# Moving the scan of later batches, its decay matmul, pair 2's loads and four half tiles in a fused state-space and feed-forward kernel

One core of a Trainium2 chip. The metric is the device time of one execution in microseconds (us); the profiled span is about 1.7 us shorter than it. In the views PE is TensorE (PEld its weight loads), DVE is VectorE, ACT is ScalarE, POOL is GpSimd and SP the queue that issues most loads; to turn means to transpose, to evict means to copy a result out of PSUM, and a load lands when its last byte is there.

## The reference

Two stages. The first is a chunked state-space scan over `x, a, B, C` (4 batches, 8 heads, 768 steps, head width 32, state width 16); the second is a gated feed-forward layer over its output, turned to 3072 tokens by 256.

```python
cum = np.cumsum(la, axis=-1)                       # la = log of the decay a, per chunk
M = np.einsum('bhin,bhjn->bhij', Cc, Bc) * np.exp(cum_i - cum_j) * causal
y = einsum(M, xc) + einsum(Cc, state) * np.exp(cum)
state = exp(sum(la)) * state + sum_j(Bc * xc * exp(cum_last - cum))
...
gate = np.maximum(x @ w_gate, 0.0)                 # 256 -> 1536
return (gate * (x @ w_val)) @ w_out                # 1536 -> 256
```

## The kernel before

Tokens go in pairs of 128-token chunks (`p` = 0 to 11). Pairs 0 and 1 belong to batch 0 and must be through before the feed-forward layer has anything to do; pairs 2 and 3 are done between its tiles. For each pair: scale B and C by decay factors, turn them on PE, G = C·B on PE, mask G on DVE, then D = masked G times x on PE, then evict y into `yT`. The decay factors of batch 0 come from a short scan (`cp0`, `fac`), those of the later batches from a 384-long scan of `a_sb` and fp32 matmuls (`decay`). `gvh` is one half tile of gate and value (256 tokens), `gv` a full one; f0 to f5 are the half tiles of tiles 0 to 5. `keep_warm` puts matmuls on zeros into PE's queue, to keep it busy.

```python
    def load_bc(p, j, *qs):
        ...
            if p == 2:
                nc.vector.memset(s["bcr"][0:1, 0, 1, 0, 0:1], 0.0)   # holds the load back
        ...                                                          # till VectorE is here
    def gmask(p, q, eng, psum=False):
        eng.tensor_tensor(out=d, in0=s["gp"][q] if psum else d, in1=m, op=ALU.mult)
    ...
    # front (cut)
    d = factors();  decays(0);  keep_warm(8)
    nc.vector.tensor_copy(wfac[:, 1], d)
    nc.vector.memset(wg[0:1, 0, 0:1], 0.0)        # holds the weight loads back
    weights(0, 2);  weights(2, 4);  weights(4, 6, (0,))
    scale_wide(0, 1, V)
    ...
    scan(0, H)                                     # ahead of pair 0's masks
    scale_wide(1, 1, P_);  scale_wide(1, 0, P_)
    weights(4, 6, (1,))
    ...
    D_wide(0, (2, 3, 0));  D_wide(0, (1,))
    turn(1, True);  keep_warm(2)
    yevac_wide(0, A_, V)
    load_bc(2, 1, nc.sync);  load_bc(2, 0, nc.sync)     # <- pair 2's C and B, here
    carry(0, 1)
    weights(6, 8);  weights(8, NF)
    weights_out(0, NF // 2);  weights_out(NF // 2, NF)
    tevac(1, V, A_);  cast_x(1, V);  pass_on(0, 1)
    f0 = gvh(0, 0, 0, True)
    G_wide(1)
    decay()
    adds(1)
    ...                                            # masks, carry, f0()
    late = [gvh(0, f, 0, True) for f in (1, 2, 3)]
    inter_wide(1);  D_wide(1)
    late[0]();  late[1]()
    yevac_wide(1, A_, V)
    late += [gvh(0, f, 0, True) for f in (4, 5)]
    ...
    scale_wide(2, 1, P_);  scale_wide(2, 0, P_)    # GpSimd, then its masks and memsets
    ...
    halves(0, 1, 0, 1, 2, 3, 4, 5)
    gv(0, 6);  carry(1, 1);  gv(0, 7);  load_x(2, nc.sync);  load(3)
    ...
    gv(0, 8);  turn(2)
```

## Time and profile before

| | before |
|---|---|
| time, median of the first 3 runs | 124.58 us (124.43 to 124.73) |
| profiled span | 122.7 us |
| PE's share of the chain that ended last | 92% |
| PE without a hole from | 14.87 us |
| second halves of the first tiles start | 15.75 us |

The prediction shows the lines that carry this. Two further views matter later. The first is the instructions on pair 2's `bcr` (its B and C) in the stretch where they are asked for: duration (min/median/max ns), first and last start, and the us from issue to landing.

```profile
L89 SPq DMA_DIRECT2D bcr<-in_C_dram x1: 368/368/368, 10.4 to 10.4; - x1
L89 SPq DMA_DIRECT2D bcr<-in_B_dram x1: 995/995/995, 10.8 to 10.8; - x1
DMA to landing us min/median/max: 3.5/4.3/5.2
```

They are issued at 10.4 and 10.8 and are there by 16. The second is busy time by stretch (stretch, length, then busy us and count of PE, weight loads, DVE, ACT and POOL, then granted clock, DMA share, GB/s):

```profile
22.00:24.00 2.00, 2.00 (x12) 0.97 (x11) 1.43 (x4) 1.73 (x4) 0.65 (x2) 1.00 1.14 210
32.00:34.00 2.00, 2.00 (x50) 1.73 (x48) 2.00 (x6) 1.83 (x6) 1.75 (x3) 1.00 0.96 120
```

PE is full in both.

### The profile page before, as it was taken

Reading aid. Unit: us, or ns where it says so; the run is one execution under the profiler, and the core shown is the slowest. Engines: PE = TensorE matmul, PEld = TensorE weight load, DVE = VectorE, ACT = ScalarE, POOL = GpSimd, SP = SyncE. Lnnn points to the kernel's source line nnn. Section 1 sums busy time; section 2 is a strip of 40 time slices with the busy share of each in tenths; the row PEclk is TensorE's granted clock in tenths of the full one; section 3 lists DMA queues with packets and bytes.
Section 4 is the critical chain, followed back from the end, with each engine's and each line's share of the span. In section 5 each row is a group of like instructions: output and inputs, shape, how many; then the busy total and the mean of one; then the engine's idle time right before and its main releaser. Section 6 shows DMA issues by size and latency. Waiting matters only on the chain.

```text
span 122.7 us, 3665 instructions
## 1 busy us (share of the span) xinstructions
PE 118.1 (96%) x1404; PEld 82.4 (67%) x1404; DVE 88.0 (72%) x200; ACT 76.3 (62%) x169; POOL 48.2 (39%) x108
## 2 busy tenths in 40 slices
PE   6989999999999999999999999999999999999990
PEld 6856784577875478874577864677854678844790
DVE  4798988872799864988763897855987656788410
ACT  0467688835987725786635886545877447876420
POOL 6499989361455127360351806033600033000000
DMA  3999999996979995999999498960580002200022
GB/s 63 220 208 146 171 192 194 189 172 103 115 89 139 143 142 143 103 150 205 150 114 140 154 136 138 110 117 0 189 52 0 0 0 91 85 0 0 0 91 86
DMA packets 77489, 13.93 MB, mean 113 GB/s; under 512 B 70064, under 2 KB 77472, under 8 KB 77472
## 3 DMA queue, kind: packets, MB, share of 16 engines
q1 hardware_dynamic: 70128, 10.61, 54.2%
q0 software_dynamic: 4288, 2.36, 14.1%
q10 hardware_dynamic: 3056, 0.72, 2.7%
q8 instruction: 11, 0.18, 0.6%
q14 instruction: 6, 0.05, 0.1%
HBM read 11.13 MB, written 3.15 MB: 116 GB/s over the span
## 4 chain that ended last, share of the span: by engine, by line
PE 92%; POOL 4%; DVE 1%; issue 1%; DVEq 0%
PE o L713 26%; PE gv L686 21%; PE gate L668 15%; PE val L671 15%; PE y L643 2%; PE g L548 2%; PE w L189 2%; POOL wg L199 2%; POOL bs L322 1%; PE y L632 1%; PE o L707 1%; PE A_ps L601 1%; PE g L418 1%; POOL wv L199 1%; PE y L523 1%; PE dec L262 1%
## 5 line engine op out<-in xcount | busy, mean ns | idle before, releaser
L675 DVE TENSOR_TENSOR h<-r,val 128x512 bf16<-128x512 bf16 x44 | 30.0, 685 | 7.3 <-ACT r L674 7.2
L713 PE MATMUL o<-wo,h 128*128 128x256 bf16 x276 | 33.1, 273 | 0.0
L674 ACT ACTIVATE r<-gate 128x512 bf16<-128x512 f32 x44 | 26.3, 597 | 9.7 <-PE gate L668 9.3
L713 PEld LDWEIGHTS <-h 128*128 128x128 bf16 x276 | 25.9, 98 | 5.3 <-issue 1.7
L668 PE MATMUL gate<-yT,wg 128*128 128x512 bf16 x88 | 26.2, 379 | 0.0
L671 PE MATMUL val<-yT,wv 128*128 128x512 bf16 x88 | 26.2, 379 | 0.0
L692 DVE TENSOR_TENSOR h<-r,gv 128x256 bf16<-128x256 bf16 x56 | 22.5, 419 | 2.6 <-ACT r L689 1.8
L689 ACT ACTIVATE r<-gv 128x256 bf16<-128x256 f32 x56 | 21.2, 386 | 2.3 <-PE gv L686 0.2
L686 PE MATMUL gv<-yT,wg 128*128 128x256 bf16 x112 | 21.5, 273 | 0.0
L686 PE MATMUL gv<-yT,wv 128*128 128x256 bf16 x112 | 21.4, 273 | 0.0
L556 POOL TENSOR_SCALAR_AFFINE_SELECT gs<-gs 128x512 bf16<-128x512 bf16 (+1 forms) x16 | 8.0, 523 | 30.0 <-ACT gs L567 30.0
L573 DVE TENSOR_TENSOR gs<-g,maskUT 128x512 bf16<-128x512 f32 x16 | 10.3, 685 | 11.4 <-issue 5.6
L338 POOL TENSOR_TENSOR tok<-bcr,scaleBC 128x128 bf16<-128x128 f32 x32 | 12.2, 409 | 14.1 <-DMA bcr<-in_B_dram 13.0
L671 PEld LDWEIGHTS <-wv 128*128 128x128 bf16 x88 | 8.6, 98 | 10.4
L668 PEld LDWEIGHTS <-wg 128*128 128x128 bf16 x88 | 8.6, 98 | 8.9
L686 PEld LDWEIGHTS <-wv 128*128 128x128 bf16 x112 | 11.0, 98 | 1.3
L686 PEld LDWEIGHTS <-wg 128*128 128x128 bf16 x112 | 10.2, 98 | 1.9 <-DVE yT L536 0.2
L567 ACT CAST gs<-g 128x512 bf16<-128x512 f32 x8 | 4.7, 589 | 6.7 <-PE g L548 6.7
L656 ACT CAST yT<-y 128x512 bf16<-128x512 f32 x8 | 4.7, 586 | 5.1 <-PE y L643 2.5
L433 DVE TENSOR_TENSOR gs<-g,wmask 128x512 bf16<-128x512 f32 x9 | 5.9, 680 | 2.6 <-PE g L418 2.6
L189 PE MATMUL w<-warm 128*128 128x128 bf16 x49 | 5.5, 284 | 1.1 <-DVE tmask L163 1.1
L189 PEld LDWEIGHTS <-warm 128*128 128x128 bf16 x58 | 5.0, 126 | 1.7 <-DVE tmask L163 1.1
(122 smaller groups left out, 115.8 us busy)
## 6 DMA issues: line engine op xcount, KB each, us to landing
xr<-in_x_dram SPq DMA_DIRECT2D x17, 128.0 KB, 3.2
out_dram<-ob SPq DMA_DIRECT2D x3, 512.0 KB, 3.2
bcr<-in_C_dram SPq DMA_DIRECT2D x17, 64.0 KB, 2.9
bcr<-in_B_dram SPq DMA_DIRECT2D x17, 64.0 KB, 2.9
out_dram<-ob SPq DMA_DIRECT2D x4, 256.0 KB, 3.5
xr<-in_x_dram SPq DMA_DIRECT2D x3, 256.0 KB, 4.1
wo<-in_moe_w_out_dram POOLq DMA_DIRECT2D x2, 384.0 KB, 8.5
wg<-in_moe_w_gate_dram POOLq DMA_DIRECT2D x4, 128.0 KB, 4.0
```

Source lines behind the costliest of these rows:

```text
L189: nc.tensor.matmul(out=w, lhsT=warm, rhs=rhs, start=True, stop=True)
L338: eng.tensor_tensor(out=dst[:, t, j * (1 + t)], in0=src[:, j, :, t], in1=f[:, j, :, 4 * t:4 * t + 4].to_broadcast([128, 2, 4, N]), op=ALU. ...
L556: nc.gpsimd.affine_select(out=dst, in_=dst, pattern=[[0, n], [1, 128]], compare_op=ALU.is_ge, fill=0.0, base=0, channel_multiplier=-1)
L573: nc.vector.tensor_tensor(out=d[:, q], in0=g[q], in1=m, op=ALU.mult)
L668: nc.tensor.matmul(out=g, lhsT=wg[:, k, fs], rhs=yT[:, k, tk], start=(k == 0), stop=(k == 1))
L671: nc.tensor.matmul(out=v, lhsT=wv[:, k, fs], rhs=yT[:, k, tk], start=(k == 0), stop=(k == 1))
L674: nc.scalar.activation(r, g, AF.Relu)
L675: nc.vector.tensor_tensor(out=fst[b][:, f], in0=r, in1=v, op=ALU.mult)
L686: nc.tensor.matmul(out=gv_[:, j], lhsT=w[:, k, fs], rhs=yT[:, k, tk], start=(k == 0), stop=(k == 1), skip_group_check=True)
L689: nc.scalar.activation(r, gv_[:, 0], AF.Relu)
L692: nc.vector.tensor_tensor(out=fst[b][:, f, u * 256:(u + 1) * 256], in0=r, in1=gv_[:, 1], op=ALU.mult)
L713: nc.tensor.matmul(out=o[:, ts % 2], lhsT=fst[b][:, f, ts * 128:(ts + 1) * 128], rhs=wo[:, f], start=(f == 0), stop=(f == NF - 1), skip_gr ...
```

## The change

As the diff reads, it means to take the long scan off DVE ahead of pair 0's masks and put it into DVE's waits; to take the fp32 decay matmuls out of the stretch before pair 1's D; to fill that stretch with half tiles f1 to f4 instead, f1 in the PSUM bank that the turns use; and to do tile 5 as a full tile. The diff, cut to its core:

```diff
-    a_sb = glob.tile([2 * BH, H], FP32)                 # before x(0) on the queue
-    nc.sync.dma_start(out=a_sb, in_=a.rearrange(...))
+    a_sb = glob.tile([RL, H], FP32)                     # 48 rows, batches 1 to 3
     load_x(0, nc.sync, nc.scalar)
     load_bc(1, 1, nc.sync)
     load_bc(1, 0, nc.scalar)
+    nc.sync.dma_start(out=a_sb, in_=a[1:].rearrange(...))
@@ decay: d3 in two matmuls of 128 columns instead of four of 64; 48 columns for 64
@@ middle
-        nc.vector.tensor_scalar_mul(pick[:, 0], pairs[:, 0], rmid)
+        nc.scalar.mul(pick[:, 0], pairs[:, 0], rmid)
@@ front
-    keep_warm(8)
-    nc.vector.tensor_copy(wfac[:, 1], d)
+    keep_warm(6)                                        # weight loads asked for before this
     scale_wide(0, 1, V)                                 # now reads fac in PSUM
-    nc.vector.reciprocal(wfac[:, 0, :, :, 0], wfac[:, 1, :, :, 0])
+    nc.vector.reciprocal(wfac[:, 0, :, :, 0:2], fac[:, :, :, 0:2])
+    nc.scalar.copy(out=wfac[:, 1], in_=fac)
...
-    scan(0, H)
+    cast_x(0, A_)
     scale_wide(1, 1, P_)
     scale_wide(1, 0, P_)
-    weights(4, 6, (1,))                                 # all six now ahead of scale_wide(1)
+    cast_x(1, P_)
@@ pair 0's masks: two from ScalarE copies (bf16) instead of one
-    middle()
+    scan(0, H // 2)
...
     yevac_wide(0, A_, V)
-    load_bc(2, 1, nc.sync)
-    load_bc(2, 0, nc.sync)
+    tevac(1, None, A_)
     carry(0, 1)
+    copy_B(1, V)
+    scan(H // 2, H)
     weights(6, 8)
     ...
     G_wide(1)
-    decay()
     adds(1)
     gcopy(1, 0)
-    gmask(1, 2, V, True)
-    f0()
+    gmask(1, 3, V, True)
     gcopy(1, 1)
-    gmask(1, 3, V, True)
+    gmask(1, 0, V)
+    gcopy(1, 2)
+    load_bc(2, 1, nc.sync)
+    load_bc(2, 0, nc.sync)
     carry(1, 0)
-    ...
-    late = [gvh(0, f, 0, True) for f in (1, 2, 3)]
+    gmask(1, 1, V);  pass_on(0, 1);  f0();  pass_on(1, 0);  gmask(1, 2, V);  middle()
+    late = [gvh(0, 1, 0, True, mm.tile(..., tag="tp", name="gv1"))]
+    late += [gvh(0, f, 0, True) for f in (2, 3, 4)]
+    late[0]()
     inter_wide(1)
     D_wide(1)
-    late[0]()
     late[1]()
     yevac_wide(1, A_, V)
-    late += [gvh(0, f, 0, True) for f in (4, 5)]
+    decay()
...
-    halves(0, 1, 0, 1, 2, 3, 4, 5)
-    gv(0, 6)
+    halves(0, 1, 0, 1);  decay_factors();  halves(0, 1, 2, 3, 4)
+    carry(1, 1);  gv(0, 5);  gv(0, 6)
```

More of the change, by code (lines that the diff above doesn't have):

```diff
@@ L138 @@
     load_bc(0, 0, nc.sync, nc.scalar)
-    a_sb = glob.tile([2 * BH, H], FP32)
-    nc.sync.dma_start(out=a_sb, in_=a.rearrange("b h (w s) -> (b h w) s", w=2))
+    RL = 2 * (NB - 1) * NH
+    a_sb = glob.tile([RL, H], FP32)
     load_x(0, nc.sync, nc.scalar)
@@ L143 @@
     load_bc(1, 0, nc.scalar)
+    nc.sync.dma_start(out=a_sb, in_=a[1:].rearrange("b h (w s) -> (b h w) s", w=2))
     load_x(1, nc.sync)
@@ L176 @@
     cp0 = glob.tile([R, 128], FP32)
-    pick = const.tile([2 * BH, 2, BH], FP32)
-    pairs = identf.rearrange("p (h w) -> p w h", w=2)
+    pick = const.tile([RL, 2, RL // 2], FP32)
+    pairs = identf[0:RL, 0:RL].rearrange("p (h w) -> p w h", w=2)
     nc.vector.tensor_copy(pick[:, 1], pairs[:, 1])
@@ L232, in decays @@
         nc.scalar.copy(out=dec, in_=d)
-    cp = glob.tile([2 * BH, H], FP32)
-    rmid = const.tile([2 * BH, 1], FP32)
+    cp = glob.tile([RL, H], FP32)
+    rmid = const.tile([RL, 1], FP32)
     def scan(s0, s1):
@@ L238, in scan @@
             out=cp[:, s0:s1], data0=a_sb[:, s0:s1],
-            data1=zero1.to_broadcast([2 * BH, s1 - s0]),
+            data1=zero1[0:RL].to_broadcast([RL, s1 - s0]),
             initial=cp[:, s0 - 1:s0] if s0 else 1.0, op0=ALU.mult, op1=ALU.add)
@@ L249, in decay @@
     def decay():
-        bank_ = mm.tile([128, HC * 2 * NB * 8 + 16], FP32, tag="tp", name="dec")
-        n = HC * 2 * NB * 8
-        d = bank_[:, 0:n].rearrange("p (k w b h) -> p k w b h", k=HC, w=2, b=NB)
-        st["dec3"] = d3 = bank_[:, n:n + 16].rearrange("p (r h) -> p r h", r=2)
-        for r in range(2):
-            for i in range(2):
-                nc.tensor.matmul(
-                    out=d3[64 * i:64 * i + 64, r], lhsT=cp[:, i * 128 + r:i * 128 + 128:2],
-                    rhs=pick[:, 0, NH:2 * NH], start=(r == 0), stop=True,
-                    tile_position=(0, 64 * i), skip_group_check=True)
+        n = HC * 2 * (NB - 1) * NH
+        bank_ = mm.tile([128, n + 2 * NH], FP32, tag="tp", name="dec")
+        d = bank_[:, 0:n].rearrange("p (k w b h) -> p k w b h", k=HC, w=2, b=NB - 1)
+        st["dec3"] = d3 = bank_[:, n:].rearrange("p (r h) -> p r h", r=2)
+        turned = cp[:, 0:256].rearrange("p (i m r) -> p r i m", i=2, r=2)
+        for r in range(2):
+            nc.tensor.matmul(
+                out=d3[:, r], lhsT=turned[:, r], rhs=pick[:, 0, 0:NH], start=(r == 0),
+                stop=True, skip_group_check=True)
         for k in range(HC):
@@ L274, in decay_factors @@
             nc.scalar.copy(
-                out=scaleBC[:, :, cs, 1, :].rearrange("p b k h -> p k b h"), in_=d[:, :, w])
+                out=scaleBC[:, 1:, cs, 1, :].rearrange("p b k h -> p k b h"), in_=d[:, :, w])
     def inverse(b0, b1):
@@ L319, in scale_wide @@
         src = s["bcr"].rearrange("s (t q) j r n -> s j r t q n", t=2)[:, j]
-        f = wfac[:, j, :, :, p]
+        f = fac[:, :, :, 0] if p == 0 and j else wfac[:, j, :, :, p]
         for t in range(2):
@@ L371, in tevac @@
         s = st[p]
-        tp = s.pop("tp")
+        tp = s["tp"]
+        if beng is None:
+            s["CT"] = CT = att.tile([128, 2, 2, 128], BF16, tag="CT", name="CT")
+            for t in range(2):
+                nc.scalar.mul(
+                    CT.rearrange("s t i m -> s t (i m)")[:, t].rearrange(
+                        "s (m r) -> s m r", r=2),
+                    tp[1].rearrange("s r m -> s m r"), tmask[:, t:t + 1])
+            return
         s["BT"] = BT = att.tile([128, 2, 128], BF16, tag="BT", name="BT")
@@ L477, in carry @@
             nc.vector.scalar_tensor_tensor(
-                out=n, in0=T_.pop(c - 1), scalar=dec[:, c - 1:c], in1=st[p]["A"][i],
+                out=n, in0=T_[c - 1], scalar=dec[:, c - 1:c], in1=st[p]["A"][i],
                 op0=ALU.mult, op1=ALU.add)
@@ L675, in gv, with gvh @@
         nc.vector.tensor_tensor(out=fst[b][:, f], in0=r, in1=v, op=ALU.mult)
-    def gvh(b, f, u, later=False):
+    def gvh(b, f, u, later=False, where=None):
         if f == 0 and u == 0:
@@ L682, in gvh @@
         fs = slice(f * 128, (f + 1) * 128)
-        gv_ = bank("gv", (128, 2, 256))
+        gv_ = where or bank("gv", (128, 2, 256))
         for j, w in ((0, wg), (1, wv)):
@@ L768 @@
     keep_warm(22)
-    d = factors()
+    fac = factors()
+    nc.vector.memset(wg[0:1, 0, 0:1], 0.0)
+    for f in (0, 2, 4):
+        weights(f, f + 2)
     decays(0)
-    keep_warm(8)
-    nc.vector.tensor_copy(wfac[:, 1], d)
-    nc.vector.memset(wg[0:1, 0, 0:1], 0.0)
-    weights(0, 2)
-    weights(2, 4)
-    weights(4, 6, (0,))
+    keep_warm(6)
     scale_wide(0, 1, V)
-    nc.vector.reciprocal(wfac[:, 0, :, :, 0], wfac[:, 1, :, :, 0])
+    nc.vector.reciprocal(wfac[:, 0, :, :, 0:2], fac[:, :, :, 0:2])
+    nc.scalar.copy(out=wfac[:, 1], in_=fac)
     scale_wide(0, 0, V)
@@ L783 @@
     tevac(0, A_, V)
-    nc.vector.reciprocal(wfac[:, 0, :, :, 1:3], wfac[:, 1, :, :, 1:3])
-    scan(0, H)
+    cast_x(0, A_)
     scale_wide(1, 1, P_)
     scale_wide(1, 0, P_)
-    weights(4, 6, (1,))
-    keep_warm(6)
+    cast_x(1, P_)
+    keep_warm(4)
     G_wide(0)
     keep_warm(7)
+    adds(0)
     gcopy(0, 0)
     gmask(0, 2, V, True)
-    keep_warm(5, st[0]["gw"][:, 0, 0, 0])
-    cast_x(0, A_)
+    keep_warm(5)
+    gcopy(0, 1)
+    gmask(0, 0, V)
     decays(1)
-    adds(0)
+    keep_warm(4, st[0]["gw"][:, 2, 0, 0])
+    gmask(0, 1, V)
+    keep_warm(4, st[0]["gw"][:, 1, 0, 0])
     gmask(0, 3, V, True)
-    keep_warm(4, st[0]["gw"][:, 3, 0, 0])
-    gmask(0, 0, V)
-    gmask(0, 1, V, True)
     pass_on(0, 0)
     carry(0, 0)
-    middle()
+    scan(0, H // 2)
     inter_wide(0)
-    D_wide(0, (2, 3, 0))
-    D_wide(0, (1,))
+    D_wide(0, (2, 0, 1))
+    D_wide(0, (3,))
     turn(1, True)
@@ L817 @@
     weights_out(NF // 2, NF)
-    tevac(1, V, A_)
-    cast_x(1, V)
-    pass_on(0, 1)
+    f0 = gvh(0, 0, 0, True)
     def halves(b, u, *fs):
@@ L823, in halves @@
             gvh(b, f, u)
-    f0 = gvh(0, 0, 0, True)
     G_wide(1)
-    decay()
     adds(1)
     gcopy(1, 0)
-    gmask(1, 2, V, True)
-    f0()
-    gcopy(1, 1)
-    gmask(1, 3, V, True)
-    carry(1, 0)
+    gmask(1, 3, V, True)
+    gcopy(1, 1)
+    gmask(1, 0, V)
+    gcopy(1, 2)
+    load_bc(2, 1, nc.sync)
+    load_bc(2, 0, nc.sync)
+    carry(1, 0)
+    gmask(1, 1, V)
+    pass_on(0, 1)
+    f0()
     pass_on(1, 0)
-    gmask(1, 0, V)
-    gmask(1, 1, V)
-    late = [gvh(0, f, 0, True) for f in (1, 2, 3)]
+    gmask(1, 2, V)
+    middle()
+    late = [gvh(0, 1, 0, True, mm.tile([128, 2, 256], FP32, tag="tp", name="gv1"))]
+    late += [gvh(0, f, 0, True) for f in (2, 3, 4)]
+    late[0]()
     inter_wide(1)
     D_wide(1)
-    late[0]()
     late[1]()
     yevac_wide(1, A_, V)
-    late += [gvh(0, f, 0, True) for f in (4, 5)]
+    decay()
     for fin in late[2:]:
         fin()
-    decay_factors()
+    nc.vector.reciprocal(wfac[:, 0, :, :, 2], wfac[:, 1, :, :, 2])
     scale_wide(2, 1, P_)
@@ L861 @@
                           wmask.rearrange("p k (m r) -> p k r m", r=2))
-    halves(0, 1, 0, 1, 2, 3, 4, 5)
+    halves(0, 1, 0, 1)
+    decay_factors()
+    halves(0, 1, 2, 3, 4)
+    carry(1, 1)
+    gv(0, 5)
     gv(0, 6)
-    carry(1, 1)
     gv(0, 7)
```

## The prediction

> **What bounds the kernel now.** I read the chain of work first, then the table of busy times by stretch, then the timeline of the first 17 us engine by engine.
>
> The chain of the page, by engine:
>
> ```profile
> PE 92%; POOL 4%; DVE 1%; issue 1%; DVEq 0%
> ```
>
> TensorE is 92% of what sets the end. The table by stretch shows where it is gapless (columns: stretch, length, then busy us and count of PE, weight loads, DVE, ACT, POOL, granted clock, DMA share, GB/s):
>
> ```profile
> 0.00:10.44 10.44, 8.80 (x147) 6.95 (x148) 7.92 (x34) 4.06 (x10) 7.78 (x21) 1.00 1.04 166
> 10.44:14.87 4.43, 4.43 (x114) 3.33 (x113) 4.00 (x11) 3.40 (x10) 4.43 (x7) 1.00 1.16 147
> 14.87:119.80 104.93, 104.87 (x1158) 72.11 (x1146) 75.76 (x155) 68.83 (x150) 35.98 (x82) 1.00 0.68 108
> ```
>
> From 14.87 us on PE runs 105 us without a hole, and the change removes nothing from that part. So the change can only move the moment at which PE enters it, and how much work is still to be done then. That moment is set by a chain over DVE, ACT and POOL. The timeline shows its links (start, duration, engine, line, operation, tiles, count):
>
> ```profile
> 4.19 0.21 DVE L772 COPY wfac<-fac 128x48 f32<-128x48 f32 x1 [0.69 <-PE fac L217]
> 6.39 0.89 DVE L237 TENSOR_TENSOR_SCAN cp<-a_sb,zero 64x384 f32<-64x384 f32 x1
> 7.21 1.25 DVE L433 TENSOR_TENSOR gs<-g,wmask 128x512 bf16<-128x512 f32 x2
> ...
> 8.78 0.68 DVE L433 TENSOR_TENSOR gs<-g,wmask 128x512 bf16<-128x512 f32 x1
> ...
> 9.92 0.37 ACT L540 CAST yT<-y 128x256 bf16<-128x256 f32 x1 [0.91 <-PE Aps L523]
> ...
> 10.19 0.84 ACT L385 ACTIVATE CT<-tp,tmask 128x256 bf16<-128x256 bf16 x2
> ...
> 11.05 0.19 PEld L418 LDWEIGHTS <-BT 32*64 32x64 bf16 x16 [0.21 <-DVE BT L392]
> ...
> 11.44 0.32 PEld L257 LDWEIGHTS dec<-pick,cp 64*64 64x64 f32 x8 [0.20 <-issue]
> ...
> 11.78 0.74 PEld L262 LDWEIGHTS dec<-pick,cp 64*128 64x128 f32 x6
> ...
> 13.72 0.96 ACT L689 ACTIVATE r<-gv 128x256 bf16<-128x256 f32 x3
> ```
>
> Pair 0's G was done by about 6.85, but its first mask began at 7.21 because the 384-long scan held DVE from 6.39. The masks end at 9.46, D at 9.9. Pair 1's C-copies on ACT then run to 11.03, and G of pair 1 starts at 11.05. From there PE is fed all the time: G, the fp32 decay matmuls (11.44 to 12.59, 1.15 us), adds, f1 to f3, then D until 14.87. f4 and f5 (0.87 us) cover the eviction of y, and the second halves start at 15.75. These two times, 11.05 and 15.75, are what I compare with.
>
> **What the Trainium skill says.** "VectorE: DVE Perf Modes" (What auto-detection actually checks): a two-operand tensor operation runs at two elements a cycle only where all its tensors are 16-bit. The trace agrees: a mask from PSUM (fp32) takes 0.685 us, one from the bf16 copy 0.418. "TensorE: Matmul & The Clock Gate" (Architectural detail: the array is 16× 32×32): ACT and DVE queues are strict FIFO. My case rests on this; in the trace ACT's and DVE's instructions indeed stand one after another in program order. The same page (LDWEIGHTS): the time of a weight load goes by its columns. The trace agrees: the six fp32 loads of 128 columns take 0.74 us (0.123 each), the eight of 64 columns 0.32 (0.04 each). So fewer rows (48 for 64) make decay no cheaper.
>
> **The change, part by part, up to pair 1's G.** "Step" below is the distance from one start to the next on its engine, as the timeline has it: mask from PSUM 0.58 to 0.61, mask from bf16 0.38 to 0.40, ACT copy of G 0.48, relu of a half tile 0.38, Sw 0.25 to 0.32, carry 0.19.
> - The copy of fac goes to ACT and the scale reads PSUM: bs(C) starts at 4.19 for 4.43 (-0.24). The reciprocal is 32 long for 16 (0.34 for 0.25), so bs(B) ends at 5.35 for 5.61, and G of pair 0 starts at 6.16 for 6.42 (-0.26).
> - DVE has no scan before the masks: first mask at 6.62 for 7.21. ACT now does the cast of x first (6.1 to 6.72, x having landed) and two copies (6.68 and 7.16). The DVE masks go 6.62, 7.32, 7.8, 8.2 and end at 8.88 for 9.46 (-0.58): two of them are bf16 for one.
> - dec, Sw and inter on ACT and PE come at 8.06, 8.2, 8.6. D runs 8.83 to 9.45 for 9.9 (-0.45). The first half scan sits in DVE's wait for D (8.78 to some 9.3).
> - ACT evicts y at 9.5 and makes C of pair 1 by 10.71 for 11.03. POOL starts its weights at about 3.7 for 4.73, but has six for five (0.72 each), and ends the scales at 9.9 for 10.23; its cast of x is 0.61. So G of pair 1 starts at 10.75 for 11.05: **the front gives 0.30 us**. The second half scan fits into DVE's wait for that G.
>
> **From G to the second halves.** G is readable at 11.25.
> - ACT: copies at 11.25, 11.73, 12.21, Sw at 12.69 and 12.93, free at 13.28. The multiplication of pick now stands here and waits for the reciprocal on DVE.
> - DVE: masks at 11.30 and 11.90, carry 12.33, mask 12.52, f0 12.90, mask 13.24, reciprocal 13.62 to 13.76.
> - ACT again: pick 13.80, relu f1 to f4 at 14.0, 14.38, 14.76, 15.14. Only then, as its queue is FIFO, does it evict y: 15.52 to 15.89, though D is done at some 14.2 (inter at 13.35 after Sw, D at 13.7 after the last mask).
> - PE: adds 11.2, f1 11.4 (turn bank), f2 to f4 to 13.15 in banks that the G evictions free (11.85 to 12.3). It idles some 0.7 us before D is complete.
> - decay takes the turn bank, so it waits for DVE's finish of f1 (14.42 to 14.83). Ten fp32 loads of 128 columns at 0.135: 1.35 us, 14.87 to 16.2.
> - The second halves start at 16.25 with yT since 15.94.
>
> So they start 0.50 later than at 15.75, and f5 is still wholly ahead (four matmuls of 256 columns at 0.109: 0.44 us; a full tile is two halves, so "six full" or seven is the same PE work). **Sum: +0.94 us.** PE's own work between G and the second halves is the same or more (decay 1.35 for 1.15, f4 before D and f5 left for later); what decay used to do in the mask wait is done after D, where eviction has to be waited for anyway, but ACT and DVE get more than they can do by then. My handoffs are full ones in a row and errors there mostly go one way, so I take off a third and predict 125.2 us.
>
> **Rivals.**
> - *Everything fits and PE stays fed.* Then the halves start after G 0.34, adds 0.28, five f less f0 1.75, inter and D 0.7, decay 1.35 = 4.42 after 10.75, at 15.17, with 0.44 more to do: -0.14 us, and -0.4 with a better front: 124.2 to 124.45. For it: ACT had 0.84 us idle before Sw at 13.46. Against: pick and four relus together are 1.7 us on ACT before the eviction.
> - *f2 gets f0's bank.* The five shared banks are all held at that time (four by G, one by f0), and f0's finish is moved behind three masks. If banks are handed out in rotation, f2 waits until 13.3, D ends at 15.3, decay at 16.7: +1.3 us or more, 126. Against: the turn bank is used for f1 alone, as if the rest found banks.
> - *The later bcr load* (its gate moves from 10.33 to about 12.3) *or a later decay_factors delays pair 2 or 3.* The former has slack (turn of pair 2 at 21.13; landing 5 us at most). Pair 3's chain of loads begins on DVE at 21.1 as before, with G at 30.76 without a hole; if it fell behind, +0.3.
> - *The front gives nothing*, as the weights asked for 1 us earlier slow the loads of B, C and x in a stretch with 210 GB/s: G at 11.05, +1.2 us in all.
>
> **Range and chances.** The stall-free case is the floor, 124.2; the bank case the ceiling, near 126. The middle chain has most of the weight. Gains or losses of 2% (2.5 us) are outside all rivals: the front before G is only 11 us and the rest is dense. Predicted 125.2, range 124.2 to 126.0; faster 0.01, same 0.97, slower 0.02.
>
> **What would show it.** Right: first mask of pair 0 near 6.6, G of pair 1 near 10.75, ACT's eviction of pair 1's y behind four relus at 15.5, decay starting only after f1's finish near 14.9 and lasting 1.35, a PE hole of over 0.5 us between f4 and D and another after D, the second halves near 16.2, then gapless to the end. Wrong: decay directly behind D, or the second halves before 15.5, or D much earlier than 14.2; or a hole in PE after 17 us.

## The result, and the profile after

The changed kernel took 128.85 us in the median of 4 runs (127.86 to 130.10, the last slow), the kernel before 124.66. Ratio of fast runs 1.0304, 95% interval 1.0231 to 1.0376: **slower by 3%**. (A ratio is the mean time of one kernel's fast runs over that of the other's of the same rounds, so not quite the ratio of the medians.) Executions over 1.5% slower than the fastest of the same kernel are left out of the means. The profiled run took 127.86 us, span 126.2 against 122.7, that is +3.5 us.

The chain that ended last, by engine, of the changed kernel:

```profile
PE 76%; POOL 10%; DMA 4%; DVE 4%; issue 3%; ACT 1%; DVEq 0%; ACTq 0%; POOLq 0%
```

PE went from 92% to 76%, POOL from 4% to 10%, and the DMA came in. To see where, set the two timelines of PE side by side at the same work:

| PE reaches | before | after | later by |
|---|---|---|---|
| G of pair 1 (weight load) | 11.05 | 10.91 | -0.14 |
| decay's first weight load | 11.44 | 14.96 | |
| gate of tile 6 | 18.38 | 19.29 | +0.91 |
| turn of pair 2, first half | 20.96 | 21.88 | +0.92 |
| gate behind that turn | 21.19 | 23.34 | +2.15 |
| first output matmul | 23.78 | 25.93 | +2.15 |
| G of pair 3 | 30.69 | 34.10 | +3.41 |
| end of the span | 122.7 | 126.2 | +3.5 |

The front costs 0.91 us; the rest comes after 21 us, 1.24 us at the turn of pair 2 and 1.26 us between it and pair 3's G, and almost nothing after 34. The timeline of the front in the changed kernel, for the steps that the prediction gave a time to:

```profile
10.91 0.16 PEld L427 LDWEIGHTS <-BT 32*64 32x64 bf16 x16 [0.21 <-DVE BT L406]
...
13.88 0.31 ACT L246 ACTIVATE pick<-identf,rmid 48x24 f32<-48x24 f32 x1 [0.45 <-DVE rmid L245]
...
14.10 1.16 ACT L698 ACTIVATE r<-gv 128x256 bf16<-128x256 f32 x4
...
14.96 0.54 PEld L259 LDWEIGHTS dec<-pick,cp 48*128 48x128 f32 x4 [0.64 <-DVE h L701]
...
15.15 0.36 ACT L549 CAST yT<-y 128x256 bf16<-128x256 f32 x1
...
15.43 0.74 PEld L263 LDWEIGHTS dec<-pick,cp 48*128 48x128 f32 x6
...
16.23 0.11 PEld L695 LDWEIGHTS <-wg 128*128 128x128 bf16 x2
```

decay waits 0.64 us for DVE's finish of f1, then takes 1.3 us; the second halves start at 16.24. Now the second part. The same two stretches of busy time as before:

```profile
22.00:24.00 2.00, 0.94 (x9) 0.43 (x7) 0.96 (x4) 0.68 (x2) 1.47 (x6) 1.00 0.61 110
32.00:34.00 2.00, 1.17 (x11) 0.80 (x9) 0.31 (x1) 0.57 (x2) 0.00 (x0) 1.00 0.55 106
```

PE idles about 1 us in each. What it waits for there, in the timelines of PE and of GpSimd, the changed kernel first:

```profile
18.52 0.78 POOL L323 TENSOR_TENSOR bs<-bcr,wfac 128x128 bf16<-128x128 f32 x2 [3.35 <-DMA bcr<-in_C_dram]
...
22.38 0.78 POOL L323 TENSOR_TENSOR bs<-bcr,wfac 128x128 bf16<-128x128 f32 x2 [3.08 <-DVE fac L882]
...
23.21 0.28 PE L368 MATMUL tp<-ident,bs 128*128 128x128 bf16 x2 [1.06 <-POOL bs L323]
...
34.10 0.42 PE L427 MATMUL g<-turned 32*64 32x256 bf16 x16 [0.93 <-DMA turned<-tok]
```

In the kernel before, GpSimd scales pair 2 without a wait, and further down its row has a reserve:

```profile
15.45 1.53 POOL L322 TENSOR_TENSOR bs<-bcr,wfac 128x128 bf16<-128x128 f32 x4
...
24.84 0.61 POOL L350 CAST xb<-xr 128x512 bf16<-128x512 f32 x1 [2.19 <-DMA xr<-in_x_dram]
```

And the loads of pair 2 in the changed kernel:

```profile
L89 SPq DMA_DIRECT2D bcr<-in_C_dram x1: 367/367/367, 12.5 to 12.5; - x1
L89 SPq DMA_DIRECT2D bcr<-in_B_dram x1: 582/582/582, 13.0 to 13.0; - x1
DMA to landing us min/median/max: 5.8/7.6/9.3
```

They are issued 2.1 us later, but C lands at 18.3 and B at 22.3. GpSimd's scaling of B starts at 22.38, PE's turn at 23.21. Behind that scaling, in GpSimd's row, stand the memsets of masks and tokens (5.7 us), the cast of x and the scaling of pair 3. The scaling of pair 2 ends 6.2 us later than before (23.16 for 16.98), more than the 2.19 us for which GpSimd waited there; so pair 3's turn by DMA is issued at 31.20, and PE stands still again before its G. A third wait, of 0.21 us at 29.42, is for the late cast of x.

The label of the second GpSimd wait ("<-DVE fac L882") is a trap: that reciprocal happens to end at 22.28, and the label names what came last by the profile. The DVE operation whose result the instruction reads, the reciprocal of `wfac`, ran at 16.15; and in after_again's trace the same wait bears the name of another ("<-DVE xr L97", a one-element memset).

### The profile page after: what moved, and what is told of

Its sections match the earlier page's. It is cut to its first block, busy times and chain, and to the rows that moved or that the text cites. A ratio compares the mean times of both kernels' runs of the same rounds, so it can differ in the third digit from the quotient of the medians.

```text
span 126.2 us, 3645 instructions
## 1 busy us (share of the span) xinstructions
PE 118.0 (94%) x1390; PEld 81.7 (65%) x1396; DVE 87.0 (69%) x197; ACT 77.2 (61%) x172; POOL 49.1 (39%) x109
## 4 chain that ended last, share of the span: by engine, by line
PE 76%; POOL 10%; DMA 4%; DVE 4%; issue 3%; ACT 1%; DVEq 0%; ACTq 0%; POOLq 0%
PE o L722 20%; PE gv L695 18%; PE val L680 14%; PE gate L677 13%; DMA turned<-tok 2%; PE y L652 2%; PE g L557 2%; POOL bs L323 2%; POOL wg L200 2%; POOL tok L869 2%; DMA a<-in_a_dram 1%; POOL tok L311 1%; DVE gs L442 1%; PE y L641 1%; POOL wv L200 1%
## 5 line engine op out<-in xcount | busy, mean ns | idle before, releaser
L684 DVE TENSOR_TENSOR h<-r,val 128x512 bf16<-128x512 bf16 x45 | 30.7, 684 | 8.7 <-ACT r L683 8.5
L683 ACT ACTIVATE r<-gate 128x512 bf16<-128x512 f32 x45 | 26.9, 597 | 10.0 <-PE gate L677 9.5
L680 PE MATMUL val<-yT,wv 128*128 128x512 bf16 x90 | 26.8, 379 | 0.3
L677 PE MATMUL gate<-yT,wg 128*128 128x512 bf16 x84 | 25.5, 379 | 0.0
L701 DVE TENSOR_TENSOR h<-r,gv 128x256 bf16<-128x256 bf16 x54 | 21.6, 418 | 4.0 <-ACT r L698 3.4
L698 ACT ACTIVATE r<-gv 128x256 bf16<-128x256 f32 x54 | 20.3, 384 | 3.7 <-PE gv L695 2.0
L695 PE MATMUL gv<-yT,wg 128*128 128x256 bf16 x108 | 20.8, 273 | 0.0
L695 PE MATMUL gv<-yT,wv 128*128 128x256 bf16 x108 | 20.6, 273 | 0.2 <-DMA wv<-in_moe_w_val_dram 0.2
L582 DVE TENSOR_TENSOR gs<-g,maskUT 128x512 bf16<-128x512 f32 x16 | 10.3, 686 | 11.4 <-issue 5.6
L576 ACT CAST gs<-g 128x512 bf16<-128x512 f32 x8 | 4.7, 589 | 6.7 <-PE g L557 5.1
L442 DVE TENSOR_TENSOR gs<-g,wmask 128x512 bf16<-128x512 f32 x7 | 4.6, 686 | 4.2 <-PE g L427 4.2
L446 ACT CAST gs<-g 128x512 bf16<-128x512 f32 x9 | 4.8, 591 | 2.2 <-PE g L427 2.2
```

The costliest lines, as they stand in the source:

```text
L582: nc.vector.tensor_tensor(out=d[:, q], in0=g[q], in1=m, op=ALU.mult)
L677: nc.tensor.matmul(out=g, lhsT=wg[:, k, fs], rhs=yT[:, k, tk], start=(k == 0), stop=(k == 1))
L680: nc.tensor.matmul(out=v, lhsT=wv[:, k, fs], rhs=yT[:, k, tk], start=(k == 0), stop=(k == 1))
L683: nc.scalar.activation(r, g, AF.Relu)
L684: nc.vector.tensor_tensor(out=fst[b][:, f], in0=r, in1=v, op=ALU.mult)
L695: nc.tensor.matmul(out=gv_[:, j], lhsT=w[:, k, fs], rhs=yT[:, k, tk], start=(k == 0), stop=(k == 1), skip_group_check=True)
```

## The experiments

Theory T: the later issue puts pair 2's loads among the weight loads; they land late, and both PE holes follow. Rival R1: GpSimd waited for DVE, as the label says. Rival R2: all loads are slower, as the first six weight loads are asked for 1 us earlier.

### early_bc

```diff
     yevac_wide(0, A_, V)
+    load_bc(2, 1, nc.sync)
+    load_bc(2, 0, nc.sync)
...
     gcopy(1, 2)
-    load_bc(2, 1, nc.sync)
-    load_bc(2, 0, nc.sync)
```

> The changed kernel with one thing undone: the two loads of pair 2's B and C are issued again where the kernel before issues them (behind pair 0's eviction, about 10.4 us) and not at 12.5. Theory T (the later issue puts these loads among the weight loads, they land 6 to 9 us later instead of 3.5 to 5, and the turn of pair 2 and then GpSimd's whole row of work up to pair 3's G come late): landing within 5.5 us, no PE hole at the turn of pair 2 nor before pair 3's G, and only the loss of the front left, +0.9 us: 125.3 to 125.9 us. Rival R1 (GpSimd waited for VectorE, whose decay factors now come later, as the profile's label of that wait says): the holes stay, over 127.5 us. Rival R2 (all loads are slower as six weight loads are asked for 1 us earlier): the loads still take over 6 us, about 127 us.

Fast runs 125.39, 125.60, 125.64 us; ratio 1.0061 (0.9993 to 1.013). That is T's number; R1 and R2 would have left it at 127 or more. But two of five runs took 127.70 and 127.76, and the profile fell on one of those. In it pair 0's eviction came only at 11.45, so the loads went out at 11.96 and 12.37, in spite of the old place in the program, and took 5.6 and 8.4 us. PE, itself over 2 us late in that run, had no hole at either place. So this trace does not show the early issue. That second kind of run is taken up below.

### late_bc_only

```diff
-    load_bc(2, 1, nc.sync)                # behind yevac_wide(0)
-    load_bc(2, 0, nc.sync)
...
     f0()
     gcopy(1, 1)
+    load_bc(2, 1, nc.sync)
+    load_bc(2, 0, nc.sync)
     gmask(1, 3, V, True)
```

> The kernel before with that one move alone: pair 2's B and C loaded behind pair 1's f0 finish on VectorE, about 12.5 us for 10.4. T: landing 6 to 9 us, PE holes of about 1 us each at the turn of pair 2 and before pair 3's G, +2.0 to +3.0 us, so 126.6 to 127.7 us. R1 and R2: within 0.3 us of the kernel before, as nothing else is changed.

Fast runs 129.25 and 130.48 us, ratio 1.0401 (1.0311 to 1.0492). The move alone costs the kernel before at least as much as the whole change does: the direction is T's, but the loss is 4% and not the 2% that I expected (3.4% for 129.25, the one run at a full clock; 130.48 has a mean clock of 0.985). Its loads and PE's turn of pair 2 (the profile is of a slow run; it is quoted for the waits, not for the time):

```profile
L89 SPq DMA_DIRECT2D bcr<-in_C_dram x1: 367/367/367, 13.1 to 13.1; - x1
L89 SPq DMA_DIRECT2D bcr<-in_B_dram x1: 582/582/582, 13.5 to 13.5; - x1
DMA to landing us min/median/max: 9.1/10.4/11.8
```

```profile
23.14 0.29 PE L367 MATMUL tp<-ident,bs 128*128 128x128 bf16 x2 [1.58 <-POOL bs L322]
26.25 0.39 PE L367 MATMUL tp<-ident,bs 128*128 128x128 bf16 x2 [2.83 <-POOL bs L322]
```

Issued half a microsecond later than in the changed kernel, right ahead of the output weights, the loads take 9.1 and 11.8 us, and PE waits 4.4 us at the turn alone. Before pair 3's G there is no second hole, unlike what I expected: PE is late enough by then. In this trace the hole also costs more than its length: the granted clock is 0.60 in 24 to 26 us, 0.50 from 26 to 30 and 1.00 again from 32, and from the turn to the first output matmul PE needs 4.95 us (26.44 to 31.39) for 2.59 in the changed kernel.

### wo_later

```diff
-    weights_out(0, NF // 2);  weights_out(NF // 2, NF)       # behind weights(8, NF)
     scale_wide(2, 0, P_)
+    weights_out(0, NF // 2);  weights_out(NF // 2, NF)
```

> The changed kernel, with the two loads of the output weights (768 KB) asked for by GpSimd only behind its scaling of pair 2. If they are what the late B and C loads compete with: B lands within 5 us of its issue at 12.96, GpSimd's second scaling starts before 18.5 (22.38 in the changed kernel) and there is no hole at the turn of pair 2; instead PE waits at the first output matmul, since the output weights land 8 to 9 us after about 18, near 27. If the loads are slow for another reason, landing stays over 8 us. The time itself says little: 126 to 129.

A half miss: the two loads took 6.7 and 6.8 us (5.8 and 9.3 in the changed kernel), where I had expected under 5 for B. There was no hole at the turn, and PE waited at the output matmuls, as expected; GpSimd's scaling started at 19.93, not before 18.5. The one run took 132.62 us. So the output weights are only part of the competing traffic.

### weights_behind

```diff
-    weights(6, 8);  weights(8, NF)
-    weights_out(0, NF // 2);  weights_out(NF // 2, NF)
     scale_wide(2, 0, P_)
+    weights(6, 8);  weights(8, NF)
+    weights_out(0, NF // 2);  weights_out(NF // 2, NF)
```

> The changed kernel with all weight loads that GpSimd asks for between 10.6 and 15.2 us (gate and value weights from tile 6 on, and the output weights, 1.5 MB) put behind its scaling of pair 2. With the output weights alone put back, pair 2's B still took 6.7 us and not the 5 that I had expected, so the gate and value weights should be the rest. If traffic of weights is what delays the late loads: both land within 4 us of their issue near 12.5 to 13, GpSimd scales pair 2 by 17.5, no PE hole at its turn; PE then waits for weights from tile 6 on (the time will be 130 us or more and says nothing). If landing stays over 5.5 us, something other than the weights delays them.

With all of the later weights behind them, the loads issued at 12.74 and 13.15 land in 3 us:

```profile
L89 SPq DMA_DIRECT2D bcr<-in_C_dram x1: 367/367/367, 12.7 to 12.7; - x1
L89 SPq DMA_DIRECT2D bcr<-in_B_dram x1: 582/582/582, 13.1 to 13.1; - x1
DMA to landing us min/median/max: 2.9/3.0/3.0
```

So the same late issue takes 3.0 us, or 5.8 to 11.8, and the only edit between is where the weight loads stand. T's account of the landing is shown; that the loss follows from it, early_bc and late_bc_only show. (PE then waits for weights; 130.74 us, as was to be. This run and wo_later's are single ones of unknown state, with mean clocks of 0.984 and 0.973; up to 20 us, where the loads land, the granted clock is 1.00 in both.) The Trainium skill, "DMA: Bandwidth & Descriptors" (Queues, rings and completion order), says that each DMA engine takes turns between rings packet by packet; that B and C's 128-byte rows get a small share of such turns would fit, but no run here separates it from plain queueing.

### after_again

The changed kernel unaltered, five rounds.

> The changed kernel unaltered, for its spread on one chip and a second trace. The late loads of pair 2's B and C are a race with weight loads, so their landing differs from run to run (9.1 and 11.8 us in the kernel that only has the late loads): time between 127.5 and 130 us; in the trace again a PE hole at the turn of pair 2 and one before pair 3's G, over 1.8 us together.

Fast runs 128.36 to 129.78 us, ratio 1.0348 (1.0302 to 1.0395), two more at 130.3 and 130.6 (slow). The trace is of one of the slow runs: the loads issued at 14.69 and 15.11 took 9.6 and 9.8 us, and there are holes of 1.02 and 0.45 us at the turn and of 0.93 us before pair 3's G, as expected. The first trace, at 127.86, is thus one of the changed kernel's best runs.

### early_bc_warm

```diff
-    keep_warm(6)          # behind factors
+    keep_warm(8)
...
-    keep_warm(4)          # ahead of G_wide(0)
+    keep_warm(6)
```
on top of early_bc.

> early_bc had two kinds of runs, 125.4 to 125.6 and 127.7 us, and its trace of a 127.7 shows PE at half speed up to 13.6 us (the same keep-warm matmul 314 ns long for 219). Here it gets back the four warm matmuls that the change took from the stretch before pair 0's G (8 and 6 for 6 and 4). If these are what releases the clock in time: all runs at 125.3 to 126. If the release is a matter of chance in each run: two kinds of runs again. In a trace of a fast run the loads land within 5.5 us, and PE has no hole at the turn of pair 2 and none before pair 3's G.

Fast runs 125.31, 126.00 and 126.70, ratio 1.0118 (1.0055 to 1.018), but three of six at 127.6 to 127.7: restoring the warm matmuls does not remove the second kind of run. (These three have a mean clock of 0.986, early_bc's two 1.000, so they need not be the same kind.) The profile is of the fast run of 126.0, and gives what early_bc's could not. Its loads, and the same two stretches:

```profile
L89 SPq DMA_DIRECT2D bcr<-in_C_dram x1: 368/368/368, 10.8 to 10.8; - x1
L89 SPq DMA_DIRECT2D bcr<-in_B_dram x1: 582/582/582, 11.2 to 11.2; - x1
DMA to landing us min/median/max: 3.3/3.7/4.0
```

```profile
22.00:24.00 2.00, 2.00 (x14) 1.05 (x13) 1.54 (x5) 1.79 (x5) 1.41 (x3) 1.00 0.18 31
32.00:34.00 2.00, 2.00 (x45) 1.44 (x44) 1.24 (x3) 1.75 (x5) 0.65 (x1) 1.00 1.00 117
```

Landing is back at 4 us and both holes are gone. In this run the gate of tile 6 starts at 19.78 (+1.40 against before) and pair 3's G at 32.15 (+1.46); the span is +1.5. The front's loss is carried to the end, and nothing is added to it. It is larger than the changed kernel's 0.91; in this run the warm matmuls are at full rate only from about 7.3 us, in the changed kernel's trace from about 5.

### decay_shared

```diff
-        bank_ = mm.tile([128, n + 2 * NH], FP32, tag="tp", name="dec")
+        bank_ = bank("decs", (128, n + 2 * NH))
```
on top of early_bc.

> early_bc, and decay's matmuls write a shared bank instead of the turn bank, so they need not wait for VectorE's finish of f1. If that wait is what holds the second halves in the front, decay starts directly behind D near 14.4 (14.96 in the changed kernel), the halves start near 15.7 (16.24), and the time is 0.4 to 0.6 us below early_bc's. If the eviction behind four relus is the bound, the halves start at 16.2 as before and the time is the same.

One fast run, 124.79 us; three slow ones, 127.5 to 128.6. In the trace, of a slow run, decay starts right behind D (17.69) with no wait for f1's finish. It also shows two things that go wrong in the new front. First, DVE's bf16 masks (min/median/max ns), and GpSimd's row:

```profile
L442 DVE TENSOR_TENSOR gs<-gs,wmask x5: 414/416/2040, 7.6 to 15.8; 128x512 bf16<-128x512 bf16 x5
```

```profile
8.18 1.53 POOL L323 TENSOR_TENSOR bs<-bcr,wfac 128x128 bf16<-128x128 f32 x4
```

The mask that started at 7.97 took 2.04 us instead of 0.42 and ended only after GpSimd's four scalings. The Trainium skill, "SBUF — State Buffer" (SBUF: two separate sides), describes an exclusive lock on a pair of ports that DVE and GpSimd share, for a DVE operation with two SBUF inputs too, when GpSimd reads SBUF, and says that the one that starts first keeps the pair. The trace agrees in that the two hold each other up; it does not in who wins, for by the profile's times (rough on GpSimd) the mask began 0.21 us before the scalings. Nor is it so in each run: the same mask beside the same scalings took 0.61 us in the changed kernel's trace. In the kernel before there is one such mask of pair 0 and three that read PSUM, and it took 0.467 us. Second, while PE waited 1.41 us for that mask its granted clock fell to half, and stayed there for some 7 us (9.5 to 16.4).

### psum_masks and psum_masks_turn

psum_masks is decay_shared with pair 0's masks from PSUM again (three from PSUM, one bf16, done before GpSimd scales); psum_masks_turn is the same with decay back in the turn bank.

```diff
     gmask(0, 2, V, True)
-    gcopy(0, 1)
     gmask(0, 0, V)
-    gmask(0, 1, V)
     gmask(0, 3, V, True)
+    gmask(0, 1, V, True)
```

> decay_shared had one run of 124.8 and three of 127.5 to 128.6 us; its trace shows a bf16 mask of pair 0 on VectorE that took 2.04 us for 0.42, exactly while GpSimd ran its four scalings (8.18 to 9.71). Here pair 0's masks are again three from PSUM and one bf16, the bf16 one second, ahead of GpSimd. If the bf16 masks and GpSimd shut each other out: no mask over 0.75 us, D of pair 0 done by 9.9, most runs at 124.6 to 125.3. If the slow runs came from the PE clock alone they stay, at 127 or more.

Five fast runs, 124.68 to 125.79, one slow (126.99); ratio 1.0042 (1.0006 to 1.0077). No mask over 0.70 us in the trace, which is of the slow run. As decay_shared has one fast run, what the masks alone are worth is not shown.

> psum_masks (1.0042 of the kernel before in fast runs) with decay back in the turn bank, its only difference from early_bc being pair 0's masks. If the wait of decay for f1's finish is worth what the trace shows (0.5 us between D and decay): fast runs 0.4 to 0.6 us slower than psum_masks, ratio 1.008 to 1.010. If eviction behind four relus is the bound instead: ratio unchanged at 1.004. Slow runs: fewer than in early_bc (2 of 5), if they came of the bf16 masks beside GpSimd.

Fast runs 125.20, 125.93, 126.94 and 126.98, ratio 1.0131 (1.0079 to 1.0183); two slow. Two of the fast ones have a clock of 0.986; the other two are 1.007 of the kernel before. So the bank is worth 0.4 to 1.1 us, and the direction is that of the wait; the smaller figure is not clear of noise, and the two kernels ran in different sessions on different chips. The trace of psum_masks_turn shows decay waiting 0.40 us for f1's finish. Slow runs did not become rarer than in early_bc.

### front_only and front_lite

Two tries at a better version: the kernel before with parts of the change's front. front_only takes all of it but the 48-row scan (six weight loads 1 us earlier, GpSimd's cast); front_lite leaves GpSimd's row as it was (cut; a_sb is also loaded behind x, as in the change):

```diff
     fac = factors()
-    nc.vector.tensor_copy(wfac[:, 1], d)
     scale_wide(0, 1, V)                     # reads fac
+    nc.vector.reciprocal(wfac[:, 0, :, :, 0:2], fac[:, :, :, 0:2])
+    nc.scalar.copy(out=wfac[:, 1], in_=fac)
...
-    scan(0, H)                              # ahead of the masks
...
     carry(0, 0)
-    middle()
+    scan(0, H)
...
+    middle()                                # behind tevac(1)
     cast_x(1, V)
```

> A try at a version better than both: of the change only its front (PSUM scale, copy on ScalarE, a_sb later, scan in VectorE's wait for D, weights asked for earlier, cast of pair 1 on GpSimd), with pair 1, decay, f1 to f5 and the loads of pair 2 as in the kernel before. G of pair 1 at 10.8 to 10.9 for 11.05, PE fed from there as before: 0.1 to 0.3 us below the kernel before, if PE's clock is released in time; the same or slower if the front's gain is lost to the clock or to the masks.

A miss: 126.17 to 127.57 us in fast runs, ratio 1.0186 (1.0145 to 1.0226), which the 2% rule leaves as unclear; three of these five runs have a clock of 0.986. In its trace, of the run of 126.17, B of pair 2 is issued at 11.36 and takes 9.2 us (GpSimd's weight loads are asked for from 10.94 on), and pair 3's G waits 0.95 us. Here the loads' place in the program is that of the kernel before; with other timing around it they fall among the weights all the same.

> A second try at a better version, after front_only lost 1.9%: of the front only what leaves GpSimd's row and the loads' times as they were (PSUM scale with the copy on ScalarE, a_sb behind x, scan in VectorE's wait for D, the factor of pick behind the copy of B), all else as in the kernel before. The loads of pair 2 go out a little earlier, the bf16 mask of pair 0 ends before GpSimd's scaling starts. 124.0 to 124.5 us where the kernel before has 124.4; if the order of the loads was what cost front_only its 1.9%, this one must not show it.

Fast runs 124.35, 124.59, 125.16, ratio 1.002 (0.9978 to 1.0063), loads landing in 4.1 and 4.7 us: no loss, and no gain either. Three of six runs are slow. No version here beats the kernel before.

### The second kind of run

Of 33 runs of the kernel before one was slow; of the 49 runs of kernels with all or part of the new front 18 were. They are of more than one sort: 8 have a mean granted clock of 0.973 to 0.987, 10 one of 0.996 to 1.000. Nor does it take the new front: late_bc_only has the old one, and two of its four runs were slow (0.972 and 0.974). early_bc's trace of a 127.76 us run, recorded with a clock of 1.00 throughout, shows PE's warm matmuls (min/median/max ns, first and last start) never at full rate up to 11.8 us, where the changed kernel's fast trace has full rate from about 5 us:

```profile
L190 PE MATMUL w<-warm x50: 287/314/315, 1.1 to 11.8; 128*128 128x128 bf16 x50
```

```profile
L190 PE MATMUL w<-warm x50: 219/314/314, 1.1 to 10.3; 128*128 128x128 bf16 x50
```

As these matmuls stand ahead of the real ones in PE's queue, pair 0's D ended near 11.4 for 9.6, and the second halves started at 18.54 for 16.24. "TensorE: Matmul & The Clock Gate" (The HAM clock gate) says that the clock is released around 4 us into sustained matmul work, give or take 0.5 us, because the window that decides runs freely. The changed kernel's fast trace agrees, with full rate about 4 us after the first warm matmul at 1.06. This one does not: PE was busy for 98% of 1.0 to 11.2 us and still not at full rate. What sets the moment, and whether the new front shifts it, stays open: restoring the four warm matmuls did not help.

## Why the prediction was wrong

It gave 125.2 us, range 124.2 to 126.0, and 97% for "same" (within 2%).

- **The front was right in its mechanism, and its sum partly by luck.** Reciprocal and pick came at 13.63 and 13.88 (13.62, 13.80 predicted), decay at 14.96 for 1.28 us (14.87, 1.35), the halves at 16.24 (16.25), and +0.91 us at tile 6 (+0.94). Decay waits for f1's finish, as said, and in decay_shared's trace, with a shared bank, it does not. But the first mask came at 6.89 (6.62) and G of pair 1 at 10.91 (10.75), so the better front gave 0.14 us and not 0.30; the steps from G to the reciprocal were 0.15 us quicker than predicted and made up for it. The hole of over 0.5 us between f4 and D did not come: f4 waited 0.15 us on PE for its value weights, which the prediction had not seen, and D followed at once. The one after D did (0.47 us). The third that was taken off the sum was not there to take: +0.91 stood whole. The eviction behind four relus came at 15.15 and not 15.52, since a relu there steps by 0.26 and not 0.38; it was not the bound.
- **The weight loads were read right for rows only.** Six fp32 loads of 128 columns took 0.74 us with 64 rows before and with 48 after; but the eight of 64 columns took a third of that each (0.04 for 0.123), and not half, so time by columns fits in direction alone.
- **f2 did not get f0's bank**: it started at 12.02. That rival was rightly doubted.
- **The step that failed** is in the rivals, "The later bcr load": "The former has slack (turn of pair 2 at 21.13; landing 5 us at most)". The 5 us was read from a load issued at 10.85, ahead of most of the weights (it took 5.2). Issued at 12.96 it took 9.3 us, 11.8 when 0.5 us later still, and 3.0 with the weights out of the way. I took the landing time as a property of the load; it is one of the traffic. I had even the ingredients: DMA busy throughout in that stretch, 1.5 MB of weights asked for between 10 and 15.5 us, and in the trace of before the output weights themselves took 8.0 to 9.1 us to land.
- **A second step failed with it**: I looked only at the turn of pair 2 for that slack. GpSimd's work stands in program order in the traces, so its late scaling pushed 5.7 us of memsets and pair 3's scaling, and the second hole (0.93 us, before pair 3's G) came from there. I had asked for pair 3 only whether its loads start in time, and allowed 0.3 us. Together the two steps give the 2.5 us between +0.91 and +3.41.
- **"Gains or losses of 2% (2.5 us) are outside all rivals"** fell with them.
- Some runs add a slow clock, in the front or behind a hole. I had looked at the clock only as granted, 1.00 everywhere in the trace of before.

Undone in that one point the change gives 125.4 to 125.6 us in its fast runs, 1.006 of the kernel before (0.9993 to 1.013). That fits the front's sum, but the interval is too wide to tell 0.9 us from none.

## What to carry to other kernels

A load's time to landing is measured with the traffic of its own moment: when a change moves an issue, ask what is issued in the microseconds before and after it, and count the bytes in flight, before granting it the old landing time. And ask of a late result not only who waits for it first, but what stands behind it on the engine that makes it. A label in a table of waits names what came last; check it against what the instruction reads.

## What the Trainium skill lacked or had wrong

- "DMA: Bandwidth & Descriptors" (Queues, rings and completion order) tells of rings taking turns, but gives no figure for a small load among large ones. Here two loads of 128 KB took 2.9 to 3.0 us with 1.5 MB of weights held back, 5.8 and 9.3 us among them, and 9.1 and 11.8 us when issued just ahead of the last 768 KB.
- "SBUF — State Buffer" (SBUF: two separate sides) says that whichever starts first has the shared ports for its whole instruction and the other is blocked. Here, in one trace of decay_shared, a DVE operation of 0.42 us took 2.04 us, through four GpSimd instructions in a row (1.53 us), although it had begun 0.21 us before them.
- "TensorE: Matmul & The Clock Gate" (The HAM clock gate) calls the ramp less than 1% of a typical span, and puts its end around 4 us, give or take 0.5. In early_bc's one traced slow run the release came after 11.8 us of nearly unbroken matmuls; the two such runs took 127.7 us, 1.7% more than the fast ones.
